# A reordered schedule for a convolution and gated feed-forward kernel: new instruction order, weight sums moved, the last stores split

## The chip, the cores and the metric

The kernel runs on one core of one Trainium2 chip. The metric is the device time of one execution in microseconds, as the median of the runs shown. A core has a matrix engine (TensorE, in the profile PE, with its weight loads as PEld), three engines for elementwise work (VectorE = DVE, ScalarE = ACT, GpSimd = POOL) and queues from which DMA transfers are issued (SP, POOL and ACT issue them here). Each engine works through its own instructions strictly in the order in which the program gave them; between engines there are only semaphore waits. So the order in which the program emits instructions is the schedule.

## What is computed

Everything is in float32.

```
x: (8, 4096, 192), weight: (8 heads, 7 taps), w_gate and w_val: (192, 1536), w_out: (1536, 192), rms_g: (192)

w = softmax(weight, axis=-1)                       # 7 taps for each head of 24 channels
y[b, s, h, :] = sum_k w[h, k] * x_pad[b, s + k, h, :]      # causal, padded with 6 zero rows
t = y.reshape(32768, 192)
tn = t / sqrt(mean(t * t, -1) + 1e-6) * rms_g
g = tn @ w_gate
out = (g * sigmoid(g) * (tn @ w_val)) @ w_out
```

## The kernel before

**Pairs.** The 32768 tokens are cut into 32 pairs of blocks; a pair is 1024 tokens, two halves of 512. Pair 0 is done in the plain way, pairs 1 to 31 with a scheme that saves multiplications: instead of the products of a plain block matrix multiplication, sums of operands are multiplied and the results are added and subtracted again. For this the operands of x (`x_op`, tiles `xb` and their sums `xc`), of w_gate and w_val (`wf`) and of w_out (`wo_sb` and its sums) have to be formed.

**A pair from 1 on** takes 180 steps of TensorE ("places" in the text). The first 120 come from `CHAINS`: for each of four quarters (`Unit` u = 0 to 3) of the 1536 hidden columns, 15 products, each for two halves of the array (gate rows and value rows); line L823, 240 matmuls of 512 columns in all. The other 60 come from `OUTS` ("9.2" is product 9 of quarter 2): they multiply the gated hidden columns, or sums of them, with the forms of w_out; line L1002, eight short matmuls for a step, 480 in all. `LEFT` says which form a product reads and into which accumulator it goes: K, R, N, and C0, C1, C3, C4, which share two PSUM banks. `BANKS` says in which half of the eight banks each of them is.

**The order by hand.** `ORDER` is a list of words, walked once for each pair: "p3" emits the next three products of TensorE, any other word one instruction (or one group) on the engine that its first letter names: A = ScalarE, V, P and W = VectorE, G = GpSimd, Q = an accumulating DMA issued by GpSimd, D = DMAs from SP. A word with a trailing "-" belongs to the pair before. The words:

- `S..`, `F..`, `D5`, `C`, `N`, `R.` with half and quarter: snapshots, forks and joins of the products in PSUM (lines L772, L776, L839, L849, L857); `G.`: the silu (L869); `M.`: the gated product gate x value into `ht` (L877, on GpSimd or VectorE).
- `ab`, `cb`, `de`, `p4`, `p9`, `abe`, `bcf` and so on with a quarter: sums of gated columns (L1027; as Q a DMA, L1025). A `k` in front (`kp9`) stages the second operand in a PSUM bank by ScalarE (L726), so that VectorE (P) can do the sum.
- `X0` to `X10`: the sums `xc` of the next pair's operands (L718; as Q two DMAs, L711 and L712); `fetA`, `fetB`: the DMAs that bring these operands, `xb` (L702), with the small DMA `mark` between them.
- `cv0_1` and so on: tap 0 of 7 in third 1 of the convolution for the pair after the next (ScalarE L474 for tap 0, VectorE L482 for taps 1 to 6); they accumulate in a PSUM bank whose half `SIDE` gives. Then `sq`, `red`, `pow`, `bc`, `mul` (square, reduction on VectorE, root on GpSimd, spread on VectorE, scaling on GpSimd, L498 to L536), `place` (the scaled rows go to DRAM, L676) and `load` (x of a later pair, L158).
- `S2` to `S13`, `F0` to `F4`, `D0` to `D13` without a quarter: snapshots, forks and joins of the output accumulators (L772, L776, L1049); `T0` to `T5`: transposes into `o_sb` (L1015); `st0`, `st1`: the stores, four DMAs each (L1068).

At the end of a pair, joins and transposes are done in the next pair (the words with "-"). For the last pair the walk goes on once more with no pair of its own (`range(1, PAIRS + 1)`, `now = None`).

**The start.** `START` is a string in which each letter advances one generator of pair 0's work: "p", "s", "v" the plain products (L1110), silus (L1121) and gated products (L1128); "i" the conversion of w_gate and w_val (the inputs are float64 words, taken apart), "o" and "O" that of w_out (L335 and L336 are its last two steps, on GpSimd); "c", "n", "t" convolution, norm and `place` of pair 1; "w" the weight sums `w_sums` (L375, and L371 for the two negations of a quarter: 17 sums and 2 negations of 128 columns each, four to a step, five steps to a quarter). `LATER` puts more of these steps at times after `base`, the start of pair 0's output stage `outer` (L1151, evacuated by L1159 on ScalarE and L1163 on VectorE). The numbers are places in an emission order, not clock times: everything is kept in a heap and emitted in the order of these numbers. In the same heap are, for pair 2, the taps: the third accumulator's first tap (L474) at base + 1140, its six further taps (L482) up to base + 1640; then the sums `xc` of pair 1 (L718) from base + 1860 on; and `out_sums`, the 17 sums and one negation of w_out's forms (L914, L910), 12 steps from base + 2600 on and the other six inside pair 1, one after every tenth product.

Of the kernel before, what the change touches and what calls it, by code (L numbers as in the profile page):

```python
# [13 lines left out]
ALU = mybir.AluOpType  # L14
# [5 lines left out]
def kernel(  # L20
# [10 lines left out]
    nc = tc.nc  # L31
# [59 lines left out]
    BANKS = {'K': 1, 'R': 1, 'N': 0, 'C01': 1, 'C34': 0}  # L91
    OUTS = (
        "11.1 11.0 6.0 6.2 4.1 6.1 6.3 11.2 4.2 1.0 1.2 11.3 4.0 4.3 14.3 9.0 8.0 8.1 8.2 9.1 9.3",
        "9.2 14.2 14.1 5.0 8.3 10.0 5.3 10.3 5.1 5.2 3.1 13.2 13.1 3.3 7.0 7.3 13.0 10.1 7.1 10.2",
        "7.2 13.3 1.3 14.0 12.0 3.0 2.1 12.1 12.3 12.2 1.1 3.2 0.3 2.2 2.0 0.1 0.2 2.3 0.0",
    )
    ORDER = (
        "VD6- VD0- GX5- GX10- p1 VT2- p1 GX9- VD2- VD3- VT4- p2 VT5- Asq- AS40.0.0 p2 AS40.1.0",
        "VT3- p1 AF0.0.0 VT0- GX8- p1 VT1- VC.0.0 GX7- AF0.1.0 p3 VC.1.0 AS41.0.0 AS41.1.0 p1",
        "AS00.0.0 p2 AS00.1.0 p2 GX4- p1 Vred- VD5.1.0 AS42.0.0 VD5.0.0 p1 AS42.1.0 VR1.0.0",  # L100
        "VR0.0.0 Gpow- VR1.1.0 AS51.0.0 p1 AS51.1.0 p1 VR0.1.0 p1 Dload- Vbc- AF2.0.0 p1 AG0.0.0",
        "AF3.0.0 AG1.0.0 VN.1.0 p1 VR2.0.0 GM0.1.0 p1 AF3.1.0 p2 AG2.0.0 AS44.1.0 VR2.1.0 p2",
        "Dst1- p1 VS44.0.0 p1 VR3.0.0 p2 AS40.0.1 VR3.1.0 AS40.1.1 p1 GM1.1.0 VR5.0.0 Gmul-",
        "AG4.0.0 GM2.1.0 VR5.1.0 VM4.1.0 AG3.0.0 p1 AF0.0.1 p1 GM3.1.0 p2 Gcb.0 p1 VS41.0.1 p1",
        "AF0.1.1 VC.0.1 p1 AS41.1.1 VC.1.1 AS00.1.1 AG5.0.0 p1 VS00.0.1 p2 AS42.1.1 VS42.0.1",
        "VD5.0.1 AS51.0.1 p1 VD5.1.1 GM5.1.0 p1 AS51.1.1 p1 Gab.0 p2 VR1.0.1 p1 VR1.1.1 p1",
        "AF2.0.1 p1 AF2.1.1 VR0.0.1 p1 VR0.1.1 AG0.0.1 Qbe.0 VF3.0.1 Gdf.0 p3 VR2.0.1 GM0.1.1 p1",
        "AF3.1.1 VR2.1.1 p1 AG1.0.1 AS44.0.1 AS44.1.1 p1 VR5.0.1 AG5.0.1 GM1.1.1 p1 VR3.0.1 p1",
        "AS40.0.2 p2 VR5.1.1 VS40.1.2 p1 VR3.1.1 p2 Gde.0 p3 AG4.0.1 GM5.1.1 AF0.0.2 VM4.1.1",
        "VF0.1.2 AG3.0.1 VC.0.2 AS41.0.2 p2 VC.1.2 AS41.1.2 AG2.0.1 p1 AS00.0.2 p1 VS42.0.2 Gab.1",  # L110
        "p1 GM3.1.1 AS00.1.2 AS42.1.2 p2 VD5.0.2 p4 VD5.1.2 VR1.0.2 AS51.0.2 GM2.1.1 p1 VR1.1.2",
        "AS51.1.2 p2 VR0.0.2 AF2.0.2 p1 AF2.1.2 p1 VR0.1.2 p1 AG1.0.2 AG0.0.2 AF3.1.2 Gcb.1 p1",
        "VF3.0.2 VR2.0.2 VR2.1.2 AS44.0.2 p1 Gdf.1 Qde.1 GM1.1.2 VR5.0.2 AS44.1.2 VR5.1.2 p3",
        "AG2.0.2 p4 VR3.0.2 VS40.1.3 GM0.1.2 AS40.0.3 AG5.0.2 AG4.0.2 VR3.1.2 p1 AF0.0.3 p1",
        "AS41.0.3 p2 Gab.2 VM4.1.2 VF0.1.3 VC.0.3 p1 GM2.1.2 p1 VC.1.3 AS41.1.3 p4 GM5.1.2",
        "VS42.0.3 p1 AS00.0.3 AS00.1.3 VD5.0.3 VD5.1.3 p1 AG3.0.2 Gcb.2 AS42.1.3 p1 VR1.0.3",
        "VR1.1.3 p1 Dst0- AS51.0.3 AS51.1.3 p1 Gdf.2 Gp4.1 AF2.0.3 p1 AF2.1.3 AG1.0.3 VR0.0.3 p1",
        "VR0.1.3 p2 AF3.0.3 AF3.1.3 VS44.0.3 VR5.0.3 p1 GM3.1.2 p1 AG0.0.3 p1 AS44.1.3 VR2.0.3 p2",
        "VR5.1.3 AG5.0.3 p2 Qde.2 VR3.0.3 Qbe.2 AG4.0.3 VM4.1.3 p1 WR3.1.3 AG2.0.3 AG3.0.3 p1",
        "Akp4.2 p2 GM1.1.3 VM3.1.3 p2 GM0.1.3 Akab.3 Akp9.0 Pp4.2 p2 AS6 GM5.1.3 Pab.3 p1 WR2.1.3",  # L120
        "Gdf.3 Dplace- Akp4.0 Gde.3 Acv0_1 p2 DfetA DfetB p1 Pp4.0 p1 AF3 Gp4.3 Akp9.1 VM2.1.3",
        "Qp9.2 p1 Pp9.0 Vcv1_1 Pp9.1 Gcb.3 p1 Gp9.3 p1 Vcv2_1 AF1 p1 Vcv3_1 Vcv4_1 p2 Akabe.1",
        "Akbe.1 Vcv5_1 p1 Pabe.1 p2 Gabe.0 Gabe.2 p2 AF0 Acv0_2 Vcv6_1 p1 Qbe.3 p1 Pbe.1 p1",
        "Vcv1_2 Akbce.0 p1 Qabe.3 p1 VS8 p3 AkX3 p1 Pbce.0 p1 AS5 Vcv2_2 p1 Gbce.3 Akbcf.1 Vcv3_2",
        "PX3 p1 Gbce.2 p2 Gbce.1 Vcv4_2 p1 Vcv5_2 Vcv6_2 Acv0_0 Gbcf.0 QX0 Vcv1_0 Akabd.1 p2",
        "Pbcf.1 Qabd.0 p2 AS7 Pabd.1 p2 Vcv2_0 Gbcf.2 p1 AS13 p2 Akbcf.3 Pbcf.3 VD13 AkX6 Akabd.2",
        "p2 Qabd.3 p1 Vcv3_0 Vcv4_0 Pabd.2 Vcv5_0 p2 AF4 p1 Vcv6_0 p2 VD1 p1 GX1 p3 VD7 AS2 PX6",
        "GX2",
# [238 lines left out]
    def w_sums(u):  # L367
        t = wf[u]
        for i, (d, op, a, b) in enumerate(WSUM):
            if op == "neg":  # L370
                nc.gpsimd.tensor_scalar(  # L371
                    out=t[:, d, :], in0=t[:, a, :], scalar1=-1.0, scalar2=None, op0=ALU.mult
                )
            else:
                nc.gpsimd.tensor_tensor(  # L375
                    out=t[:, d, :], in0=t[:, a, :], in1=t[:, b, :],
                    op=ALU.add if op == "add" else ALU.subtract,
                )
            if i % 4 == 3:
                yield  # L380
        yield
# [524 lines left out]
    def out_sums():  # L906
        for d, op, a, b in VSUM:
            dst = right(d)
            if op == "neg":
                nc.gpsimd.tensor_scalar(  # L910
                    out=dst, in0=right(a), scalar1=-1.0, scalar2=None, op0=ALU.mult
                )
            else:
                nc.gpsimd.tensor_tensor(  # L914
                    out=dst, in0=right(a), in1=right(b),
                    op=ALU.add if op == "add" else ALU.subtract,
                )
            yield

    SIDE = (1, 0, 0)  # L920
# [29 lines left out]
    class Pair:  # L950
# [78 lines left out]
        def do(self, eng, name):  # L1029
# [29 lines left out]
            elif act in ("st0", "st1"):  # L1059
# [4 lines left out]
                for i in range(NQ):  # L1064
                    rows = slice(r + i // 2 * HALFT, r + (i // 2 + 1) * HALFT)
                    cols = slice(i % 2 * D // 2, (i % 2 + 1) * D // 2)
                    q = nc.scalar if i % 2 and p == PAIRS - 1 else nc.sync
                    q.dma_start(  # L1068
                        out=out[rows, cols].rearrange("(b p) d -> p b d", p=Q),
                        in_=o[i * Q : (i + 1) * Q],  # L1070
                    )
# [154 lines left out]
    def done(it):  # L1226
# [11 lines left out]
        "iwpvsicwpsiwvpisvivcpsocvpwispvswcipvwsipsiwOvpsiwvipsvvpswopsvcpsvOnovoOpsonvOpsnoOvnopso"  # L1238
# [3 lines left out]
        (463, "w"), (564, "w"), (664, "w"), (764, "w"), (864, "w"), (964, "w"), (1064, "w"),  # L1242
        (1164, "w"), (1264, "w"),
# [75 lines left out]
    later(wsum, *[base + 2600 + 60 * i for i in range(12)])  # L1319
# [4 lines left out]
    order = [w for row in ORDER for w in row.split()]  # L1324
    past = None
    for p in range(1, PAIRS + 1):
        now = Pair(p) if p < PAIRS else None
        done_to = 0
        for w in order:
            if w[0] == "p":  # L1330
                for _ in range(int(w[1:])):
                    if now:
                        next(now.line)
                    done_to += 1
                    if p == 1 and done_to > 30 and done_to % 10 == 0:
                        next(wsum, None)
# [36 lines left out]
```

## Time and profile before

| | us |
|---|---|
| median of 3 runs | 2606.48 (2603.78 to 2611.65) |
| the profiled execution | 2604.78 |
| its span, first to last instruction | 2602.9 |
| pair 0: first plain product to the end of its output stage | 28.57 to 125.3 |
| pair 1: first L823 to the first L823 of pair 2 | 125.0 to 212.3 |
| pairs 2 to 30 | 212.36 to 2516.61 |
| pair 31: to the end of its last matmul | 2516.61 to 2595.25 |
| mean of one L823 / L1002 matmul as listed | 0.59 / 0.38 |
| one sum of 128 x 512 on GpSimd / on VectorE, as listed | 1.38 to 1.53 / 0.68 |
| one weight sum L375 / L914 on GpSimd, mean | 0.729 / about 0.78 |
| one negation L371 on GpSimd, mean | 0.850 |

A listed duration holds the time in the pipeline; instructions that follow each other without a wait start closer together than that (VectorE's 0.68 at 0.60, GpSimd's 1.27 at 1.23), and matmuls overlap. TensorE's granted clock is 0.999 over the whole run. The 16 DMA engines are busy 40 to 57% of the time in the steady pairs.

### The profile page before, as it was taken

To read this page: it belongs to the slowest core of one execution; us is meant where nothing else is said; L and a number is where in the kernel's file an instruction comes from. 1 tells how busy PE (TensorE), PEld (TensorE's weight loads), DVE (VectorE), ACT (ScalarE), POOL (GpSimd) and SP (SyncE) were. 2 spreads that over 40 slices of the span, in tenths; PEclk is the share of its full clock that TensorE was granted. 3 is DMA by queue.
4 is the path that set the end of the run, shared out by engine and by line. 5 is a ranking of instruction groups with operands and counts; after the bars stand their busy time and mean duration, and the time that the engine had idled before them with its cause. 6 is when DMAs were issued, how large, how long until landed. Compare 5 with 4: busy or idle time off the path is not lost.

```text
span 2602.9 us, 61832 instructions
## 1 busy us (share of the span) xinstructions
PE 2564.1 (99%) x23128; PEld 1467.9 (56%) x23128; DVE 2424.1 (93%) x4056; ACT 1877.9 (72%) x3505; POOL 2398.9 (92%) x2104
## 2 busy tenths in 40 slices
PE   9999999999999999999999999999999999999998
PEld 6855555655555556555555555655556555645554
DVE  8889999999999999999999999999999999999976
ACT  6577777777777777677777777777778777787765
POOL 4899999999999999899999999999999999999987
PEclk9999999999999999999999999999999999999999
DMA  6243554444544445444455444455444455443432
GB/s 144 57 81 67 104 97 87 85 77 90 104 91 82 79 75 104 92 86 87 72 98 104 90 81 76 81 104 96 88 85 77 89 104 91 82 83 71 90 78 50
DMA packets 528490, 226.28 MB, mean 87 GB/s; under 512 B 456638, under 2 KB 459198, under 8 KB 528190
## 3 DMA queue, kind: packets, MB, share of 16 engines
q1 hardware_dynamic: 481004, 140.53, 27.4%
q0 software_dynamic: 44496, 81.02, 18.5%
q8 instruction: 182, 2.98, 0.5%
q10 hardware_dynamic: 2690, 0.79, 0.1%
q14 instruction: 118, 0.97, 0.1%
HBM read 83.84 MB, written 49.55 MB: 51 GB/s over the span
## 4 chain that ended last, share of the span: by engine, by line
PE 71%; POOL 15%; DMA 5%; issue 3%; DVE 2%; ACT 2%; SPq 0%; POOLq 0%; DVEq 0%; ACTq 0%
PE ps L823 51%; PE ps L1002 16%; POOL ht L877 5%; POOL nt L1027 3%; POOL early L1027 3%; PE ps L1110 2%; DMA early<-ht 2%; DMA more<-early 2%; PE ps L1151 1%; POOL tls L1027 1%; DMA xb<-xd 1%; POOL more L1025 1%; POOL more L1027 1%; ACT ps L772 0%; ACT ps L726 0%
## 5 line engine op out<-in xcount | busy, mean ns | idle before, releaser
L823 PE MATMUL ps<-xc,wf 64*128 64x512 f32 x4960 | 1398.1, 592 | 0.9 <-ACT tile L772 0.8
L823 PEld LDWEIGHTS ps<-xc,wf 64*128 64x128 f32 x4960 | 683.2, 187 | 462.4 <-issue 269.6
L823 PE MATMUL ps<-xb,wf 64*128 64x512 f32 x2480 | 864.9, 590 | 0.0
L772 ACT ACTIVATE tile<-ps 128x512 f32<-128x512 f32 (+1 forms) x749 | 416.3, 572 | 201.9 <-PE ps L1002 100.1
L823 PEld LDWEIGHTS ps<-xb,wf 64*128 64x128 f32 x2480 | 375.9, 187 | 241.0 <-issue 179.5
L772 ACT ACTIVATE ps<-ps 128x512 f32<-128x512 f32 (+1 forms) x713 | 383.1, 546 | 176.8 <-PE ps L1002 148.2
L772 ACT ACTIVATE tls<-ps 128x512 f32<-128x512 f32 (+1 forms) x615 | 344.1, 572 | 168.7 <-PE ps L1002 83.8
L877 POOL TENSOR_TENSOR ht<-ht,tile 128x512 f32<-128x512 f32 x312 | 438.8, 1471 | 22.0 <-ACT tile L869 21.1
L1002 PE MATMUL ps<-ht,x 128*32 128x256 f32 x5952 | 413.0, 380 | 0.0
L877 POOL TENSOR_TENSOR ht<-ht,tls 128x512 f32<-128x512 f32 x246 | 349.0, 1468 | 22.8 <-ACT tls L869 22.0
L1027 POOL TENSOR_TENSOR early<-early,ht 128x512 f32<-128x512 f32 x248 | 351.3, 1527 | 0.0
L482 DVE SCALAR_TENSOR_TENSOR ps<-xh,tp,ps 128x512 f32<-128x512 f32 x450 | 337.3, 751 | 15.1 <-ACT ps L474 8.8
L1027 POOL TENSOR_TENSOR early<-ht 128x512 f32<-128x512 f32 x248 | 342.7, 1382 | 4.8
L1002 PE MATMUL ps<-early,x 128*32 128x256 f32 x4216 | 278.9, 379 | 0.1
L1002 PEld LDWEIGHTS ps<-ht,x 128*32 128x32 f32 x5952 | 192.1, 110 | 130.1 <-DVE ht L877 4.9
L857 DVE TENSOR_TENSOR tile<-ps,tile 128x512 f32<-128x512 f32 x344 | 233.0, 684 | 11.0 <-ACT tile L772 6.3
L869 ACT ACTIVATE tile<-tile 128x512 f32<-128x512 f32 x344 | 213.9, 625 | 7.6 <-DVE tile L857 4.4
L857 DVE TENSOR_TENSOR ht<-ps,tile 128x512 f32<-128x512 f32 x310 | 209.9, 680 | 0.7 <-ACT tile L772 0.5
L857 DVE TENSOR_TENSOR tls<-ps,tls 128x512 f32<-128x512 f32 x276 | 187.3, 684 | 8.6 <-ACT tls L772 5.0
L726 ACT COPY ps<-ht 128x512 f32<-128x512 f32 x248 | 145.3, 589 | 60.2 <-DVE y L482 44.9
L1002 PEld LDWEIGHTS ps<-early,x 128*32 128x32 f32 x4216 | 136.6, 110 | 91.9 <-ACT ps L772 5.0
L869 ACT ACTIVATE tls<-tls 128x512 f32<-128x512 f32 x276 | 171.8, 625 | 6.0 <-DVE tls L857 3.6
(174 smaller groups left out, 3897.3 us busy)
## 6 DMA issues: line engine op xcount, KB each, us to landing
xb<-xd SPq DMA_DIRECT2D x120, 384.0 KB
ht<-ht POOLq DMA_DIRECT2D x93, 256.0 KB, 3.9
early<-ht POOLq DMA_DIRECT2D x93, 256.0 KB, 4.6
xd<-yn SPq DMA_DIRECT2D x244, 96.0 KB
out_dram<-o_sb SPq DMA_DIRECT2D x244, 96.0 KB
xh<-in_x_dram SPq DMA_DIRECT2D x192, 105.0 KB
more<-ht POOLq DMA_DIRECT2D x62, 256.0 KB, 3.3
more<-early POOLq DMA_DIRECT2D x31, 256.0 KB, 3.9
```

The costliest lines, as they stand in the source:

```text
L482: nc.vector.scalar_tensor_tensor(out=dst, in0=xk, scalar=w, in1=at, op0=ALU.mult, op1=ALU.add)
L726: nc.scalar.copy(out=bank(*at)[:], in_=src)
L772: nc.scalar.activation(out=dst, in_=src, func=AF.Copy, scale=float(s))
L823: nc.tensor.matmul(out=self.new(v, h, True) if first else self.old(v, h), lhsT=wf[self.u][HALF[h], WAT[i], :], rhs=x_op(XOP[i])[HALF[h]], ...
L857: nc.vector.tensor_tensor(out=dst, in0=self.old(v, h), in1=t[:], op=plus(s))
L869: nc.scalar.activation(out=t[:], in_=src[:], func=AF.Silu)
L877: engine[eng].tensor_tensor(out=self.hv(v), in0=src, in1=t[:], op=ALU.mult)
L1002: nc.tensor.matmul(out=to[q * Q : (q + 1) * Q, :], lhsT=left[:, u, a], rhs=cols[:, i * HALFT : (i + 1) * HALFT], start=fresh, stop=True, s ...
L1025: nc.gpsimd.dma_start(out=dst, in_=b, accum_op=ALU.add)
L1027: engine[eng].tensor_tensor(out=dst, in0=a, in1=b, op=ALU.add)
L1110: nc.tensor.matmul(out=bank(h, bks[h])[:], lhsT=wf[u][HALF[h], AT[h][k] * NF + f, :], rhs=xb[HALF[h], g, k, :], start=(k == 0), stop=(k == ...
L1151: nc.tensor.matmul(out=bank(h, bks[h])[:, w : w + D], lhsT=hts[f // NF][HALF[h], g, f % NF, j * P : (j + 1) * P], rhs=wo_sb[HALF[h], f, :] ...
```

## The change

The words of ORDER and OUTS are replaced throughout. Beside that:

- `BANKS` puts accumulators K and R into the other half, `SIDE` puts all three convolution accumulators of a pair from 3 on into the upper half.
- Several words change their engine. Sums: `p4.0`, `ab.3`, `abe.1`, `bcf.1`, `p9.2`, `de.1` and `X0` go to GpSimd; `cb.3`, `de.3`, `df.3`, `abe.2`, `abe.3`, `bcf.2` and `abd.0` to VectorE with staging; `de.0`, `be.1`, `abd.2`, `bcf.3` become DMAs. The gated products `M5` of quarters 2 and 3 go from GpSimd to VectorE.
- `fetA` moves from place 131 to 138 and `fetB` from 131 to 156; `place` from 129 to 69; `load` from 21 to 12; `st1` of the pair before from 28 to 152, between `fetA` and `fetB`; `st0` from 108 to 83.
- The two negations of each quarter of `w_sums`, and the one of `out_sums`, are done by ScalarE instead of GpSimd.
- START gets four more "w" (so that three quarters of the weight sums stand in it, not two and a fifth of the third), LATER has five instead of nine, the last at base + 864.
- All 18 steps of `out_sums` are emitted in pair 0's output stage: seven from base + 964, eight from base + 2520, three from base + 2910.
- For the last pair a new function `last` rewrites the order: each join, transpose, snapshot `S2` and store is emitted at once when what it needs (`NEEDS`) has been emitted, not in a walk after the pair; only `st1` still uses ScalarE's queue for half of its DMAs. The additional walk is gone.

```diff
-    BANKS = {'K': 1, 'R': 1, 'N': 0, 'C01': 1, 'C34': 0}
+    BANKS = {'K': 0, 'R': 0, 'N': 0, 'C01': 1, 'C34': 0}
     OUTS = (
-        "11.1 11.0 6.0 6.2 4.1 6.1 6.3 11.2 4.2 1.0 1.2 11.3 4.0 4.3 14.3 9.0 8.0 8.1 8.2 9.1 9.3",
...
-        "7.2 13.3 1.3 14.0 12.0 3.0 2.1 12.1 12.3 12.2 1.1 3.2 0.3 2.2 2.0 0.1 0.2 2.3 0.0",
+        "6.2 4.1 4.0 6.0 11.2 11.1 6.1 6.3 11.0 4.2 1.0 11.3 1.2 1.1 14.3 4.3 9.2 9.1 9.0 8.2 8.1",
...
+        "3.3 1.3 14.0 14.1 2.1 3.1 10.0 12.0 12.2 12.1 12.3 10.2 2.3 2.0 2.2 0.3 0.0 0.1 0.2",
     )
     ORDER = (
...
-        "p2 Qabd.3 p1 Vcv3_0 Vcv4_0 Pabd.2 Vcv5_0 p2 AF4 p1 Vcv6_0 p2 VD1 p1 GX1 p3 VD7 AS2 PX6",
-        "GX2",
+        "AkX3 AF4 GX0 Vcv5_2 PX3 p3 Vcv5_0 AkX6 AS2 p1 GX1 p2 Vcv6_0 VD7 Vcv6_2 GX2 PX6 GX5 p1",
+        "VT2 GX10 VD6",
     )
...
             if op == "neg":
-                nc.gpsimd.tensor_scalar(
-                    out=t[:, d, :], in0=t[:, a, :], scalar1=-1.0, scalar2=None, op0=ALU.mult
-                )
+                nc.scalar.mul(t[:, d, :], t[:, a, :], -1.0)
...
-    SIDE = (1, 0, 0)
+    SIDE = (1, 1, 1)
...
-        "iwpvsicwpsiwvpisvivcpsocvpwispvswcipvwsipsiwOvpsiwvipsvvpswopsvcpsvOnovoOpsonvOpsnoOvnopso"
+        "iwpvsicwpsiwvpisvivcpsocvpwispvswcipvwsipsiwOvpsiwvipsvvpswopsvcpsvOnovowOpsonwvOpsno"
+        "wOvnopswo"
...
-        (463, "w"), (564, "w"), (664, "w"), (764, "w"), (864, "w"), (964, "w"), (1064, "w"),
-        (1164, "w"), (1264, "w"),
+        (463, "w"), (564, "w"), (664, "w"), (764, "w"), (864, "w"),
...
-    later(wsum, *[base + 2600 + 60 * i for i in range(12)])
+    later(wsum, *[base + 964 + 80 * i for i in range(7)])
+    later(wsum, *[base + 2520 + 40 * i for i in range(8)])
+    later(wsum, *[base + 2910 + 10 * i for i in range(3)])
...
+    NEEDS = {
+        "D6": "F4 S6", "D0": "S8 F0", "D2": "S2 F4", "D3": "S2 F3", "D1": "S5 F1",
+        "D13": "S13 S6", "D7": "S7 S6", "T0": "3 D0", "T1": "10 D1", "T2": "1 D13 D7",
+        "T3": "14 D3", "T4": "0 F4", "T5": "F4 D2 D6", "st0": "T0 T1 T2", "st1": "T3 T4 T5",
+        "S2": "2",
+    }
...
+    for p in range(1, PAIRS):
+        now = Pair(p)
+        if p == PAIRS - 1:
+            order = last(order, " ".join(OUTS).split())
...
-                    if p == 1 and done_to > 30 and done_to % 10 == 0:
-                        next(wsum, None)
+                    next(now.line)
```

## The prediction

> **What bounds the kernel now.** I read the page's busy shares first, then the chain of waits in order of time, then what TensorE waited for, then timelines of one steady pair, of the first pair and of the end.
>
> ```profile
> span 2602.9 us, 61832 instructions
> PE 2564.1 (99%) x23128; PEld 1467.9 (56%) x23128; DVE 2424.1 (93%) x4056; ACT 1877.9 (72%) x3505; POOL 2398.9 (92%) x2104
> ```
>
> TensorE is 99% busy, so a new order can win only what TensorE loses; but VectorE and GpSimd stand above 90% too, so it can lose more than it wins. The chain shows each pair's first product (columns: start, length, what).
>
> ```profile
> 1005.58 37.40 PE ps L823 x170
> ...
> 1065.07 7.15 DMA more<-early
> 1072.26 17.04 PE ps L1002 x312
> 1089.30 37.19 PE ps L823 x171
> ...
> 1168.34 51.78 PE ps L823 x239
> ```
>
> From start to start this gives the pairs: 83.72 us here, then 79.04. All 29 from 212.36 to 2516.61 take 2304.25 us, 79.46 each. The 13 shortest lie at 78.74 to 79.04, mean 78.88, and in ten of them no transfer is among the chain's longest pieces; in 14 of the other 16 one is (without the 83.72 they average 79.67). The work alone is 51.78 for the 240 L823 and 480 L1002 at 17.04/312, 26.2: 78.0 us, 0.433 us for each of the 180 products ("places") of a pair. What TensorE itself waited for:
>
> ```profile
> PE ps L1002 <- POOL nt L1027: 9.8, 32, 1.3
> PE ps L1002 <- DMA more<-early: 7.1, 6, 3.0
> PE ps L1002 <- DMA early<-ht: 5.3, 8, 0.9
> ```
>
> The first is sum `p9.3` on GpSimd (0.24 us at 988.04), the others are accumulating DMAs `p9.2` and `abd.3`/`abe.3` that land late.
>
> **The steady pairs.** A DMA is safe if it is issued long before the product that reads it. Counting places in ORDER and OUTS, the shortest distances before are 7 (`de.2`), 8 (`p9.2`), 8 (`abd.3`), 10 (`be.2`); after they are 8 (`be.2`), 12, 14 (`bcf.3`), 14 (`abd.3`), 20. In the trace GpSimd runs contiguously and its real issue counts: `p9.2` is issued at 984.44, its product was due at 988.25, 3.8 us later, where the landing's median is 3.9; `abd.3` at 999.22, due at 1004.5, 5.3 against 5.1 to 6.0 on the chain. After, `p9.2` is a GpSimd sum; `bcf.3` and `abd.3` gain six places, less one or two for the queue in front, some 2 us: beyond the 6.0. `X0` becomes a GpSimd sum instead of two transfers.
>
> What this costs on GpSimd: in ORDER it has 50 sums and 9 DMA issues instead of 49 and 10. Back to back a sum takes 1.233 us (six from 967.13 to 974.54), a DMA issue about 0.75: +0.5 us a pair, against 2.3 us that it idles before the factors and the first gated product. Can it still reach `p9.3` in time?
>
> ```profile
> 936.86 1.28 POOL L877 TENSOR_TENSOR ht<-ht,tile 128x512 f32<-128x512 f32 x1 [1.25 <-ACT tile L869]
> ...
> 986.70 1.29 POOL L1027 TENSOR_TENSOR nt<-nt,early 128x512 f32<-128x512 f32 x1
> ```
>
> Before, from 936.86 to the end of `p9.3` at 987.99 are 34 sums, 5 issues and the scaling: 51.1 us. After, the same 34, 5 and the scaling stand between the start of the scaling and the end of `p9.3`. The scaling waits for VectorE's `bc`, which stands six instructions of 0.60 behind `red` (930.88, 4.2 into the pair, 2.2 long): 4.2 + 2.2 + 3.6 = 10.0. So `p9.3` ends at 61.3, and its product, one place later than before, is due at 141 x 0.433 + 0.3 = 61.4: its 0.24 us goes. `X10`, which the second product needs, then ends 12 sums and 4 issues later, 79.1 us, due at 79.9.
>
> VectorE has two sums fewer and two gated products more, ScalarE two stages fewer; both are near even. The store `st1` now stands between the halves of the fetch on SP's queue; the fetched half before it landed in 6.9 us (978.52 to 985.38), and the first use moves from place 155 to 173, 7.8 us later, which hides it. The new banks add waits that no row shows: between nothing and the 0.44 that the worst `p9.3` wait of a steady pair cost. I take nothing, because a bank is freed by rows that are already just in time.
>
> I take 78.95 a pair: the mean of the 13 shortest, with 0.07 for what is left of late transfers. 2304.25 - 29 x 78.95 = **14.7 us gained**. Ends: 78.6 (the shortest of all, the last pair: 2595.25 - 2516.61) gives 24.9; 80.26, the longest ordinary pair, costs 23.3.
>
> **The first pair.** It takes 212.36 - 125.0 = 87.4 us, 8.0 above a steady one. Six weight sums L914 of 0.73 to 1.02 push GpSimd back by some 5 us, until TensorE stands at 190.7 for the DMA behind them.
>
> ```profile
> 193.73 1.08 PE L1002 MATMUL ps<-more,wo_sb 128*32 128x256 f32 x8 [2.98 <-DMA more<-early]
> ```
>
> After, all 18 are queued before the pair begins. If the pair then runs like the others, it gains the **8.0**. But pair 0 pays. Here is GpSimd, then ScalarE, then VectorE there:
>
> ```profile
> 101.19 2.89 POOL L536 TENSOR_TENSOR yn<-y,s 128x1536 f32<-128x1536 f32 x1
> 103.96 6.52 POOL L375 TENSOR_TENSOR wf<-wf 128x128 f32<-128x128 f32 x13
> ...
> 111.54 10.49 POOL L375 TENSOR_TENSOR wf<-wf 128x128 f32<-128x128 f32 x17
> ```
>
> ```profile
> 107.64 0.69 ACT L474 ACTIVATE ps<-xh,tp 128x512 f32<-128x512 f32 x1 [7.39 <-POOL wf L375]
> ```
>
> ```profile
> 108.37 3.92 DVE L482 SCALAR_TENSOR_TENSOR ps<-xh,tp,ps 128x512 f32<-128x512 f32 x5 [0.70 <-ACT ps L474]
> ```
>
> Four more steps of `w_sums` in START put 13 sums ahead of the last conversions of w_out: 13 x 0.617 = 8.0, of which idle gaps of 2.42 and 1.96 take 4.4; GpSimd reaches L536 3.6 us later (2.1 with the 0.50 of the row at 103.96). Then come the sums of the last quarter, whose two negations are now on ScalarE, at emission time base + 864, and must wait for its 15th sum: 104.08 + 3.6 + 15 x 0.617 = 116.9 (113.7 with 0.50). Behind them in ScalarE's order is L474 at base + 1140, until now at 107.64. VectorE's third tap chain moves from 108.37 by 9 us (6), and behind it stand the sums L718 that end at 125.8 and that the first products of pair 1 need. So pair 1 starts 5.5 to 9 us later; I take 7. A TensorE that stood still also runs slower: after the 2.98 us above, 32 matmuls took 2.92 us (194.59 to 197.51) instead of 1.73, and the granted clock was 0.90 there: 1.2 us. Removing eight negations of 0.85 from GpSimd is in these figures. Net: 7 + 1.2 - 8.0, about **0**; ends -8 (the wait is covered after all) and +4.
>
> [...]
>
> **The end.** After the last matmul (2594.64 + 0.61) come a snapshot, joins and five transposes, until 2597.87, and then stores.
>
> ```profile
> 2594.89 0.38 ACT L772 ACTIVATE tile<-ps 128x256 f32<-128x256 f32 x1 [3.09 <-PE ps L1002]
> 2595.30 0.76 DVE L1049 TENSOR_TENSOR ps<-ps,tile 128x256 f32<-128x256 f32 x2 [1.23 <-ACT tile L772]
> 2596.10 1.77 DVE L1015 STREAM_TRANSPOSE o_sb<-ps 128x256 f32<-128x256 f32 x5
> 2597.24 2.10 SPq L1068 DMA_DIRECT2D out_dram<-o_sb  x4
> ```
>
> After, bank R ends four places earlier (2593.5); snapshot 0.38, two joins 0.75 and two transposes 0.8 run beside the last products to 2595.5, the last transpose ends at 2595.9, and `st0` has left already. **2.0 us gained**; ends 1 (a join waits in VectorE's order) and 3.
>
> **The sum.** -14.7 + 0 - 2.0 = -16.7 on the profiled execution's 2604.78 us (span 2602.9 and 1.9 around it): 2588.1. The median, 2606.48, is 1.7 above that execution, so I forecast **2590 us**, with 2583 to 2598 as this case's own range (steady part 8 to 20).
>
> **Rivals.** (A) Everything fits: pairs at 78.6 and the first pair's 8.0 kept: -24.9 - 8 - 2 = 2571.6 by the median. For it: the last pair does 78.64; against: only the last one, with fewer transfers. 12%.
> (B) The waits only move: GpSimd and VectorE stay above 90%, another transfer becomes the late one, the steady pairs stay at 79.46. -2.0: 2604.5. For it: `be.2` has still 8 places, and the load is the same. 22%.
> (C) Slower: VectorE becomes the bound at the start of each pair. In ORDER `cv6_0` and `cv6_2` now stand with `PX6` at place 179; before, `PX6` ended 0.14 us ahead of the first product (1005.44 against 1005.58). If VectorE runs on plan and not ahead of it, the two tap steps of 0.66 delay each pair's first product by 1.3: 29 x 1.3 = 37.7 instead of nothing, less the 14.7 and 2.0: +21, 2627. It turns slower as soon as the delay is above 0.6 us a pair. Against it: from place 166 on VectorE has 10 instructions, 5.8 us, in 14 places of 6.1 us. 16%.
> The forecast has 50%. Medians of this kernel spread so that 0.3%, 7.8 us, is about what can be told from no change: faster is below 2598.7, slower above 2614.3. The forecast lies almost wholly below, with A: 62%; B and the forecast's edge 22% the same; C 16%. The range 2573 to 2614 leaves out half of A and most of C.
>
> **What would show it.** Pair starts 78.9 apart with no `early<-ht` or `more<-early` in front of L1002 confirm the steady part; 79.4 or more means B, a wait of L823 for L718 at pair starts C. ScalarE idle before L474 near 107, and TensorE idle between L1151 and L823 near 125 to 133, confirm pair 0's price; a first pair of about 79 us its gain. The last transpose should end within 1 us of the last matmul. A steady pair above 79.3 makes the prediction wrong.

## The result, and the profile after

Timed against each other, the kernel before takes 2603.68 us (median of 12 runs) and the changed one 2608.22 (12 runs): a ratio of 1.0018, with a 95% interval of 1.0010 to 1.0025. The change costs 0.2%. The forecast was a gain of 0.6%; the loss is smaller than the 0.3% that it named as hard to tell from no change, but the interval leaves no change out.

The head of the profile after: the span, then each engine's busy time, share and instructions.

```profile
span 2607.2 us, 61944 instructions
PE 2574.3 (99%) x23128; PEld 1582.0 (61%) x23128; DVE 2427.4 (93%) x4025; ACT 1848.7 (71%) x3483; POOL 2399.5 (92%) x2095
```

The engines' shares say nothing: they are those of before. What TensorE waited for says more (columns: total us, times, longest):

```profile
PE ps L820 <- POOL xc L715: 10.6, 29, 0.4
PE ps L997 <- DVE o_sb L1010: 2.9, 2, 2.4
PE ps L820 <- DVE o_sb L1158: 2.7, 1, 2.7
PE ps L997 <- DMA ht<-ht: 2.3, 1, 2.3
```

(After the change L823 is L820, L1002 is L997, L718 is L715, L1027 is L1022, L1015 is L1010, L1163 is L1158.) The waits of the output phase are gone: before there were 9.8 us for sums of GpSimd and 12.4 for accumulating DMAs; one transfer is left. In their place stands a wait of 0.37 us in nearly every pair, for a sum of `xc` on GpSimd. Here is TensorE, then GpSimd, around the start of one pair:

```profile
769.24 1.13 PE L820 MATMUL ps<-xc,wf 64*128 64x512 f32 x4
770.74 1.13 PE L820 MATMUL ps<-xc,wf 64*128 64x512 f32 x4 [0.38 <-POOL xc L715]
771.71 1.02 PE L820 MATMUL ps<-xb,wf 64*128 64x512 f32 x4
```

```profile
750.75 1.27 POOL L1022 TENSOR_TENSOR nt<-nt,early 128x512 f32<-128x512 f32 x1
751.98 0.82 POOL L1020 DMA_DIRECT2D ht<-ht  x1
752.59 4.00 POOL L1022 TENSOR_TENSOR early<-early,ht 128x512 f32<-128x512 f32 x3
756.32 1.11 POOL L1020 DMA_DIRECT2D early<-ht  x1
756.92 3.05 POOL L1022 TENSOR_TENSOR early<-early,ht 128x512 f32<-128x512 f32 x2
759.39 2.31 POOL L1020 DMA_DIRECT2D early<-ht  x2
760.53 3.71 POOL L1022 TENSOR_TENSOR early<-early,ht 128x512 f32<-128x512 f32 x2
763.03 2.44 POOL L715 TENSOR_TENSOR xc<-xb 128x512 f32<-128x512 f32 x1
765.55 2.55 POOL L715 TENSOR_TENSOR xc<-xb,xc 128x512 f32<-128x512 f32 x2
768.04 2.65 POOL L715 TENSOR_TENSOR xc<-xc 128x512 f32<-128x512 f32 x2
```

The first row is `p9.3`. The last four groups are `X0`; `X1` and `X2`; `X5` and `X10`. `X10` ends at 770.69, and TensorE's second product, which reads it, starts at 770.74: 1.50 us behind the first. In the kernel before, and in the kernels below that have `X10` early, this distance is 0.96. So 0.54 us is lost here, of which the profile shows 0.38 as idle, because the modelled end of the first four matmuls covers the rest.

From the first product of each pair in the two timelines, the time between kernels divides like this:

| part | forecast | measured |
|---|---|---|
| start of pair 2 (212.29 before, 213.70 after) | 0 | +1.4 |
| 29 steady pairs (2304.26, 2306.52) | -14.7 | +2.3 |
| start of pair 31 to the span's end (86.35, 86.98) | -2.0 | +0.6 |
| span (2602.9, 2607.2) | -16.7 | +4.3 |

Single traces differ: with those of the experiments below, the old order's 29 steady pairs take 2304.25 to 2307.95 us in three traces, the new order's 2305.58 to 2309.31 in seven. Between them lies nothing like the 14.7 that were forecast.

A pair's product phase is the time from its first L820 to its first L997, its output phase the rest. A steady pair now has an output phase of 26.3 us, almost always (before 26.4 to 27.9, and once 31.2), and a product phase of 53.07 (before 52.19 to 52.72). What the first won, the second gave back.

### The profile page after: what moved, and what is told of

Same layout as the page of the kernel before. It is cut to its first block, busy times and chain, and to the rows that moved or that the text cites. A ratio compares the mean times of both kernels' runs of the same rounds, so it can differ in the third digit from the quotient of the medians.

```text
span 2607.2 us, 61944 instructions
## 1 busy us (share of the span) xinstructions
PE 2574.3 (99%) x23128; PEld 1582.0 (61%) x23128; DVE 2427.4 (93%) x4025; ACT 1848.7 (71%) x3483; POOL 2399.5 (92%) x2095
## 3 DMA queue, kind: packets, MB, share of 16 engines
q8 instruction: 182, 2.98, 0.5%
## 4 chain that ended last, share of the span: by engine, by line
PE 90%; POOL 6%; issue 1%; DVE 1%; ACT 1%; DMA 0%; POOLq 0%; DVEq 0%
PE ps L820 59%; PE ps L997 28%; POOL xc L715 3%; PE ps L1105 2%; POOL ht L874 1%; POOL early L1022 1%; PE ps L1146 1%; DVE xc L715 0%; DMA ht<-ht 0%; POOL more L1022 0%; ACT tls L769 0%; POOL wf L372 0%; POOL early L1020 0%; POOL tls L1022 0%; POOL nt L1022 0%
## 5 line engine op out<-in xcount | busy, mean ns | idle before, releaser
L820 PE MATMUL ps<-xc,wf 64*128 64x512 f32 x4960 | 1433.7, 595 | 14.3 <-POOL xc L715 10.6
L820 PEld LDWEIGHTS ps<-xc,wf 64*128 64x128 f32 x4960 | 716.6, 187 | 433.4 <-issue 258.3
L820 PE MATMUL ps<-xb,wf 64*128 64x512 f32 x2480 | 886.7, 589 | 0.0
L820 PEld LDWEIGHTS ps<-xb,wf 64*128 64x128 f32 x2480 | 394.6, 187 | 189.8 <-issue 152.5
L769 ACT ACTIVATE tls<-ps 128x512 f32<-128x512 f32 x681 | 375.8, 566 | 160.7 <-PE ps L820 89.1
L997 PE MATMUL ps<-ht,x 128*32 128x256 f32 x5952 | 391.0, 380 | 5.2 <-DVE o_sb L1010 2.9
L874 POOL TENSOR_TENSOR ht<-ht,tile 128x512 f32<-128x512 f32 x245 | 357.1, 1514 | 31.1 <-ACT tile L866 30.9
L1022 POOL TENSOR_TENSOR early<-early,ht 128x512 f32<-128x512 f32 x217 | 334.8, 1885 | 1.8 <-PE ps L997 1.8
L1022 POOL TENSOR_TENSOR early<-ht 128x512 f32<-128x512 f32 x248 | 322.4, 1348 | 7.3
L997 PEld LDWEIGHTS ps<-ht,x 128*32 128x32 f32 x5952 | 190.0, 110 | 152.3 <-issue 25.8
L997 PE MATMUL ps<-early,x 128*32 128x256 f32 x4216 | 262.3, 380 | 0.0
L854 DVE TENSOR_TENSOR tls<-ps,tls 128x512 f32<-128x512 f32 x314 | 212.9, 684 | 8.9 <-ACT tls L769 3.6
L854 DVE TENSOR_TENSOR tile<-ps,tile 128x512 f32<-128x512 f32 x306 | 205.5, 683 | 4.9 <-ACT tile L769 1.8
L866 ACT ACTIVATE tls<-tls 128x512 f32<-128x512 f32 x314 | 196.2, 625 | 0.0
L997 PEld LDWEIGHTS ps<-early,x 128*32 128x32 f32 x4216 | 133.9, 110 | 95.8 <-POOL early L1022 10.5
L866 ACT ACTIVATE tile<-tile 128x512 f32<-128x512 f32 x306 | 189.5, 626 | 0.0
```

The source lines that it names most:

```text
L769: nc.scalar.activation(out=dst, in_=src, func=AF.Copy, scale=float(s))
L820: nc.tensor.matmul(out=self.new(v, h, True) if first else self.old(v, h), lhsT=wf[self.u][HALF[h], WAT[i], :], rhs=x_op(XOP[i])[HALF[h]], ...
L854: nc.vector.tensor_tensor(out=dst, in0=self.old(v, h), in1=t[:], op=plus(s))
L866: nc.scalar.activation(out=t[:], in_=src[:], func=AF.Silu)
L874: engine[eng].tensor_tensor(out=self.hv(v), in0=src, in1=t[:], op=ALU.mult)
L997: nc.tensor.matmul(out=to[q * Q : (q + 1) * Q, :], lhsT=left[:, u, a], rhs=cols[:, i * HALFT : (i + 1) * HALFT], start=fresh, stop=True, s ...
```

## Experiments

All were timed in turns with the kernel before, on one chip for each group; the ratios are to it.

**What sets the pair.** Theory: GpSimd's last sums. The rival is VectorE, or the banks.

```diff
- ... p1 GX1 p2 Vcv6_0 VD7 Vcv6_2 GX2 PX6 GX5 p1 VT2 GX10 VD6
+ ... p3 Vcv6_0 VD7 Vcv6_2 GX2 PX6 GX5 p1 VT2 GX10 VD6
- VD1- Asq- VD2- GX8- ... GX9- AS40.0.0
+ VD1- Asq- VD2- GX8- ... GX9- GX1- AS40.0.0
```

> The changed kernel with one GpSimd sum of a pair's end, X1, moved behind X10, X8 and X9 (the product that reads X1 is the tenth of a pair, the one that reads X10 the second). Theory (the last sums of GpSimd set the pair): X10 ends one sum, 1.24 us, earlier; the 0.64 us that TensorE loses ahead of the second product (0.37 of it shown as idle) goes, and as the sums end 79.6 us after the pair's start, just when they are due, the product phase falls from 53.07 to about 52.4 and a steady pair from 79.35 to about 78.7: 29 pairs gain 18, the time is near 2590. Rival 1 (VectorE at the pair's start, sums PX3 and PX6 and the tap steps, or the new banks): the order of GpSimd's sums is not what is waited for; product phase and pairs stay at 53.07 and 79.35, the time at 2608. Rival 2 (the whole loop over VectorE, scaling and GpSimd sets the pair and takes up what is given): a part only, pairs between 79.0 and 79.3.

2589.24 us, ratio 0.9947 (0.9935 to 0.9960); the product phase is 52.42, a steady pair 78.7 and the mean of 29, with one late transfer, 78.89. These are the theory's numbers; both rivals fall. (In this kernel `X5` adds the `X1` of the pair before, because `X1` now follows it, so it doesn't compute the formula. The third kernel of this group has an early `X10` and the whole sum.) The other direction:

```diff
- ... GX2 PX6 GX5 p1 VT2 GX10 VD6
+ ... GX2 PX6 GX5 p1 GX8 VT2 GX10 VD6
- VD1- Asq- VD2- GX8- VT5-
+ VD1- Asq- VD2- VT5-
```

> The changed kernel with one more GpSimd sum, X8, moved ahead of X10 (the same work, X10 one sum later). Theory (TensorE's second product waits for X10, and nothing else takes it up): the wait grows from 0.64 by the sum's 1.24 us, product phase 54.3, pairs 80.6, 29 pairs cost 36 us: 2644. Rival (the loop gives it back, since GpSimd idles 2.2 us before the scaling): pairs below 80.0, the time below 2628.

2641.88 us, ratio 1.0143 (1.0129 to 1.0157); pairs of 80.5, mean 80.68, product phase 54.18. This is TensorE's wait in that kernel:

```profile
939.93 1.13 PE L820 MATMUL ps<-xc,wf 64*128 64x512 f32 x4 [1.48 <-POOL xc L715]
```

1.1 us more on the wait for a sum of 1.24 more ahead of it. Nothing downstream takes it up: `red` starts 5.9 us into a pair here, 4.8 in the changed kernel, so the whole chain that leads to the next `X10` shifts with the late product; the idle time that GpSimd has (0.81 us before the factors, 1.42 before the scaling in the pair from 689.87) lies at another place of the pair and can't help.

`X10` can also come early with `X1` still ahead of `X5`: `X3`, on which `X5`, `X6` and `X10` build, goes into the place of `X9`, so that `X10` no longer overwrites what `X5` reads:

```diff
-        (0, 1, 4), (1, 2, 6), (2, 0, 6), (9, 3, 5), (3, 3, 8), (4, 7, 15), (5, 4, 15), (6, 5, 7),
-        (7, 0, 1), (8, 1, 2), (9, 8, 15),
+        (0, 1, 4), (1, 2, 6), (2, 0, 6), (8, 3, 5), (3, 3, 8), (4, 7, 14), (5, 4, 14), (6, 5, 7),
+        (7, 0, 1), (8, 1, 2), (9, 8, 14),
- ... GX1 p2 Vcv6_0 VD7 Vcv6_2 GX2 PX6 GX5 p1 VT2 GX10 VD6
+ ... GX2 p2 Vcv6_0 VD7 Vcv6_2 GX10 PX6 GX1 p1 VT2 GX5 VD6
```

> The changed kernel with X10 third among GpSimd's last sums (X0, X2, X10, X1, X5) and the whole sum kept: X3, on which X5, X6 and X10 build, goes into the place of X9, which is summed later, so X10 no longer overwrites what X5 reads. Theory (the last sums of GpSimd set the pair): X10 ends 2.5 us earlier, at 78.3 after the pair's start; X5 takes the end at 80.8, and the fourth product, which reads it, is due 2.6 us after the next start, at 81.3; so no wait is left at the start: product phase 52.4, pairs 78.7 to 78.9, the time 2589 to 2592. Rival (what X1 left out of its place gave was an effect of the data, or the loop takes the gain back): pairs above 79.1, the time above 2600.

2592.05 us, ratio 0.9946 (0.9933 to 0.9959), mean pair 78.94, product phase 52.43. With the changed kernel at 1.0018, the place of one sum is worth 0.7%.

**Which part of the change costs what.** Each part alone, put into the kernel before:

```diff
+ BANKS, OUTS and ORDER of the changed kernel
-    SIDE = (1, 0, 0)
+    SIDE = (1, 1, 1)
```

> The kernel before with the new steady order alone (ORDER, OUTS, BANKS, SIDE); first pair and last pair in the old way. Theory: output phases of 26.3 without a wait for a transfer, product phases of 53.07; the steady part is 2 us longer than before (29 x 79.5), the start of pair 2 as before (212), the last pair 0.7 longer by the same wait at its start: +2 to +4 us on the kernel before. If it gains more than 5 us, the loss of the changed kernel comes from the first or the last pair.

2603.34 us, ratio 0.9993 (0.9984 to 1.0001). The steady pairs are as foretold (mean 79.50, product phase 53.07), and the end is 87.27 against 86.35. The surprise is the beginning: pair 2 starts at 206.94, 5.3 us earlier than before, though nothing of the first pair's own sums was touched. Pair 1 takes 82.19 instead of 87.29. Part of this is chance in the trace of before: the last kernel of this group has the old first pair and the old order too, its pair 1 takes 83.93 us, and its pair 2 starts at 209.68, because TensorE waits 1.5 us for one DMA there and not 3.0, and its granted clock isn't halved behind that wait (before: 0.50 from 193.6 to 197.0). So pair 2 starts 2.7 to 5.3 us earlier by the new order.

```diff
+ START, LATER and places of `out_sums` of the changed kernel
-                nc.gpsimd.tensor_scalar( ... scalar1=-1.0 ... )
+                nc.scalar.mul( ... , -1.0)
```

> The kernel before with the changed first pair alone (START, LATER, the places of the weight sums, negations on ScalarE). Theory: pair 0 ends 4 to 5 us later because ScalarE's third tap waits behind two negations for GpSimd, pair 1 runs 3 us shorter; with the old order, whose first output phase then has no weight sum ahead of its transfers, pair 2 starts 0 to 2 us later than before, the rest is unchanged: 0 to +2 us. Rival (the forecast's other end): pair 1 runs at the steady 79.5 and the whole gains 3 us or more.

2611.02 us, ratio 1.0025 (1.0016 to 1.0034). Pair 1 starts at 129.17 (125.00 before), pair 2 at 214.86 (212.29); the rest is as before. The median lies beyond what these 2.6 us explain. But against the 209.68 of the other trace with the old first pair and order, pair 2 starts 5.2 us later; and the profiled run, 2607.53 us, is one of the shorter ones. The rival, a gain, falls.

```diff
+    def last(order, outs): ...
-    for p in range(1, PAIRS + 1):
+    for p in range(1, PAIRS):
```

> The kernel before with the changed last pair alone (joins, transposes and stores at once). Theory: TensorE stands before products 10 and 0, which write the other half of a bank that a transpose still reads, some 2 to 3 us in all (2.9 in the changed kernel), so the last matmul comes that much later, and the end is between 0.5 us earlier and 1 us later than before. Rival (the forecast): transposes run beside the last products and the end comes 2 us earlier.

2606.00 us, ratio 1.0006 (0.9997 to 1.0015): no gain. From the start of pair 31 to the end it takes 86.57 us, 0.2 more than before, and TensorE stands 1.98 us for a transpose ahead of its last product.

**The last pair.** This is the end of the changed kernel in its timeline, all engines: the snapshot `S2` on ScalarE, on VectorE `D2`, `T5`, `D3` and `T3`, and TensorE's last four products behind `T3`:

```profile
2598.40 0.38 ACT L769 ACTIVATE tile<-ps 128x256 f32<-128x256 f32 x1 [1.36 <-PE ps L997]
2598.82 0.43 DVE L1044 TENSOR_TENSOR ps<-ps,tile 128x256 f32<-128x256 f32 x1 [0.94 <-ACT tile L769]
2599.28 0.45 DVE L1010 STREAM_TRANSPOSE o_sb<-ps 128x256 f32<-128x256 f32 x1
2599.66 0.40 DVE L1044 TENSOR_TENSOR ps<-ps,tile 128x256 f32<-128x256 f32 x1
2600.09 0.45 DVE L1010 STREAM_TRANSPOSE o_sb<-ps 128x256 f32<-128x256 f32 x1
...
2600.69 1.93 PE L997 MATMUL ps<-ht,x 128*32 128x256 f32 x32 [2.35 <-DVE o_sb L1010]
```

`C3` and `C4` are halves of one bank (`C34`). As soon as product 2 is through, `last` queues the join `D3` and the transpose `T3` on `C3`; product 0, which writes `C4`, comes behind them and waits for both.

```diff
- ... "D3": "S2 F3", ... "T0": "3 D0", ... "T3": "14 D3", ...
+ ... "D3": "S2 F3 0", ... "T0": "3 D0 10", ... "T3": "14 D3 0", ...
```

> The changed kernel with three joins and transposes of the last pair (T0, D3, T3) held back until the products of the other half of their bank are through. Theory: TensorE's waits of 0.57 and 2.35 us ahead of the last products go, the last matmul comes 2.9 us earlier, the transposes then follow it; the end is 1 to 2.5 us earlier than in the changed kernel. Rival (the wait for a transpose is not for the bank): the 2.35 stays before the last products and the end moves less than 0.5 us.

2607.96 us, ratio 1.0001 (0.9992 to 1.0010), where the changed kernel has 1.0018. Both waits are gone, and from the start of pair 31 it takes 84.70 us instead of 86.98: 2.3 less, as the theory has it. The waits of 0.57 and 2.35 us were two products' waits for a transpose in the other half of their bank; whether the chip itself would need them was not tried.

**The first pair.** This is ScalarE at the end of pair 0 in the changed kernel:

```profile
107.12 3.49 ACTq L673 DMA_DIRECT2D xd<-yn  x4
114.31 0.51 ACT L370 ACTIVATE wf<-wf 128x128 f32<-128x128 f32 x2 [11.06 <-POOL wf L372]
114.73 0.67 ACT L471 ACTIVATE ps<-xh,tp 128x512 f32<-128x512 f32 x1
117.56 0.42 ACT L907 ACTIVATE x<-x 128x256 f32<-128x256 f32 x1 [2.16 <-POOL x L909]
117.88 0.46 ACT L1154 COPY o_sb<-ps 128x384 f32<-128x384 f32 x1
120.17 1.48 ACT L495 ACTIVATE yn<-y 128x1536 f32<-128x1536 f32 x1 [1.83 <-DVE y L479]
```

Two negations (L370) wait for GpSimd's 17 sums, and the third tap (L471), VectorE's tap chain, the square (L495) and the sums `xc` of pair 1 wait behind them. Four edits take this apart. First, the last step of the weight sums, with its negations, behind the tap:

```diff
-        ... (764, "w"), (864, "w"),
+        ... (764, "w"), (1150, "w"),
```

> The changed kernel with the step that holds the last quarter's two negations (and the sum before them) emitted behind ScalarE's third tap instead of ahead of it. Theory: the tap starts when its DMA issues end, near 110.6 instead of 114.7, VectorE's third tap chain 4 us earlier, pair 1 starts at 125 to 126.5 instead of 129.6 and pair 2 some 3 to 4 us earlier: 2604 to 2606. Rival (GpSimd's weight sums themselves, which run beside VectorE's sums, set pair 1): pair 1 starts no more than 1.5 us earlier, or pair 2's start moves less than 1.5 us.

2608.37 us, ratio 1.0004 (0.9994 to 1.0015). The tap starts at 111.41, but pair 1 only 1.6 us earlier and pair 2 too. That is just beyond the rival's 1.5 and far from the theory's 3 to 4; and five traces with the changed first pair as it is start pair 1 at 129.02 to 130.44 and pair 2 at 212.78 to 214.16, so this is little more than their spread. Now the other negation (L907) stood in front: it waited for GpSimd until 117.92, and the copy L1154 and the square (118.60) waited behind it. Next, the output weights' sums at their old places, their negation on GpSimd:

```diff
-    later(wsum, *[base + 964 + 80 * i for i in range(7)])
-    later(wsum, *[base + 2520 + 40 * i for i in range(8)])
-    later(wsum, *[base + 2910 + 10 * i for i in range(3)])
+    later(wsum, *[base + 2600 + 60 * i for i in range(12)])
```

> The changed kernel with the 18 sums of the output weights (and their one negation, on GpSimd) at their old places in pair 1; the sums of the first weights stay moved up. Theory (pair 1's slow start, a wait of 2.67 us for VectorE's o_sb, comes from the moved sums, which run beside VectorE's sums at 1.05 to 1.17 us instead of 0.72 while those take 1.10 to 1.20 instead of 0.68): VectorE's sums take 0.7 to 0.9 again, the wait of 2.67 goes, pair 1's product phase falls from 57.6 to about 54.5 and pair 2 starts at 210 to 212 instead of 213.7. Rival (only the late third tap counts): the wait stays above 2 us, pair 2 starts at 213.5 or later.

2612.19 us, ratio 1.0029 (1.0018 to 1.0040). A miss for my theory: the wait is 2.38 us, pair 2 starts at 215.55, as the rival says. The moved output sums rather help, by 1.9 us between these two traces. That VectorE's sums run beside GpSimd's in this order too, since both start late, behind the square (119.54), is my estimate; how long they take in this kernel is not shown here. Then the opposite half, the first weights' sums and negations as before, the output weights' as changed:

> The changed kernel with the sums of the first weights at their old places and their negations on GpSimd again; the output weights' sums stay moved up. Theory (the 13 weight sums ahead of pair 2's scaling and the two negations ahead of ScalarE's third tap make pair 1 late): the third tap starts before 109 us, pair 1 starts at 125 to 127.5 and pair 2 at 206 to 210 instead of 213.7: 2601 to 2605. Rival (any work moved into pair 0 costs about the same): pair 1 starts after 128.5, pair 2 after 212.

2612.55 us, ratio 1.0026 (1.0017 to 1.0035): against the theory again. The tap starts early (107.20), as it said, but the one negation left on ScalarE waits, and the rest waits behind it:

```profile
107.20 0.69 ACT L473 ACTIVATE ps<-xh,tp 128x512 f32<-128x512 f32 x1 [7.56 <-POOL wf L374]
118.86 0.42 ACT L909 ACTIVATE x<-x 128x256 f32<-128x256 f32 x1 [10.96 <-POOL x L911]
119.18 0.46 ACT L1156 COPY o_sb<-ps 128x384 f32<-128x384 f32 x1
119.54 1.49 ACT L497 ACTIVATE yn<-y 128x1536 f32<-128x1536 f32 x1
```

So either negation alone makes the square late. The last edit undoes all of them and nothing else:

```diff
-                nc.scalar.mul( ... , -1.0)
+                nc.gpsimd.tensor_scalar( ... scalar1=-1.0 ... )
```

> The changed kernel with all eight negations back on GpSimd and every sum left at its new place. Theory (each of the negations alone, queued on ScalarE ahead of the third tap or ahead of its copy into o_sb and the square, makes VectorE's sums and so pair 1 late; with one of them left, pair 1 started at 129.0 and 129.7): the third tap starts near 110.6, the square near 116 instead of 120.2, pair 1 at 125.5 to 127.5 and pair 2 at 208 to 211 instead of 213.7; the time is 3 to 5 us below the changed kernel's. Rival (the moved sums themselves make GpSimd, and so pair 1, late): pair 1 starts after 128.5, pair 2 after 212.5.

In the profile the theory's numbers come, or nearly: square 117.05, pair 1 at 127.58, pair 2 at 209.96, 3.7 us earlier. The median does not show it: 2607.19, ratio 1.0018 (1.0009 to 1.0027), as the changed kernel's. Single runs go from 2604.28 to 2614.14, and the profiled one, 2604.78, is among the three with a granted clock of 1.00; the two longest have 0.997. So the gain is shown in one trace and not in the time.

And 1.7 of its 3.7 us are the clock. In the changed kernel pair 1's product phase is 57.59 us, here 55.89. Both have the same wait of 2.67 us, for VectorE's `o_sb`, ahead of the seventh matmul. Behind it the granted clock is 0.50 from 135.5 to 138.9 us in the changed kernel, and 1.00 here. That is not tied to the negations: `e1_x1`, the first kernel of these experiments, has the changed first pair with its negations on ScalarE and that wait, and there too the clock stays at 1.00 and the phase is 55.89. The same 14 matmuls behind the wait, in the changed kernel and in `e1_x1`:

```profile
136.41 4.77 PE L820 MATMUL ps<-xc,wf 64*128 64x512 f32 x14
```

```profile
136.81 3.52 PE L820 MATMUL ps<-xc,wf 64*128 64x512 f32 x14
```

Together (the last column says for how long the granted clock is 0.50 in pair 1):

| kernel | square | pair 1 | pair 2 | half clock |
|---|---|---|---|---|
| old first pair, new order | 112.98 | 124.75 | 206.94 | none |
| all sums moved, no negation on ScalarE | 117.05 | 127.58 | 209.96 | none |
| first negations behind the tap | 118.60 | 128.04 | 212.13 | 3.41 |
| only first weights moved | 119.54 | 128.98 | 215.55 | 3.41 |
| only output weights moved | 119.54 | 129.72 | 213.67 | 3.41 |
| changed kernel | 120.17 | 129.60 | 213.70 | 3.41 |

Of the 6.8 us between the first and the last row, 2.0 are the later start of pair 1 that goes with the negations, and 1.7 the clock. The other 3.0 come with the moved sums; no kernel here moves the sums of one kind alone and leaves ScalarE without a negation. The rows point at the 13 weight sums: GpSimd's scaling (100.92 in the first kernel, 104.78 in the second) and ScalarE's third tap behind it are 3.9 and 4.1 us later.

**What beats both.** The new order with the early `X10`, and the old first and last pair:

> The kernel before with the new steady order and the early X10 of the run before this one, first and last pair in the old way. Theory: the steady gain (18 us on the steady order alone, 2603.3) without the 6.8 us by which the changed first pair starts pair 2 later: 2585, about 0.7% below the kernel before. Rival (the old first pair's weight sums collide with the earlier X10): above 2589.

2584.51 us, ratio 0.9911 (0.9897 to 0.9924). With the mended last pair as well:

> The new steady order with the early X10, the first pair in the old way, and the last pair with T0, D3 and T3 held back. Theory: the 2584.5 of the kernel without the last pair's change, less 1 to 2 us at the end: 2583. Rival: the last pair's change gives nothing, 2584.5 or more.

2581.31 us, ratio 0.9908 (0.9893 to 0.9924); the last part takes 84.09 us in place of 86.74. In the steady part this is all that the view of TensorE's waits lists, 2.4 us:

```profile
PE ps L1001 <- POOL tls L1026: 1.6, 2, 0.9
PE ps L1001 <- DMA ht<-ht: 0.8, 1, 0.8
```

With the moved sums instead of the old first pair:

> The same with the early X10 and the held back joins and transposes of the last pair: the changed kernel with its three losses mended. Theory: 18 us for the steady pairs, 2 for the end and 3 to 5 for the first pair: 2582 to 2586. It beats the version with the old first pair (2581.3) only if pair 2 starts before 207.6.

2587.17 us, ratio 0.9937 (0.9924 to 0.9950): pair 2 starts at 213.54. The moved sums don't pay in this order either. Pair 1's product phase is 58.92 here, and 55.89 with the same first pair in the changed order: behind the same wait of 2.67 us the granted clock is 0.50 for 6.83 us, from 132.3 to 139.1. Without these 3.0 us pair 2 would start near 210.5 (an estimate from these two phases), still later than the 207.60 of the kernel with the old first pair.

## Why the prediction was wrong

**The steady pairs.** The gain in the output phase was right, with its mechanism: DMAs with more places ahead of their product no longer come late (TensorE waited 12.4 us for them before, 2.3 after), and `p9.3`'s 0.24 goes. The step that failed is the next: "`X10`, which the second product needs, then ends 12 sums and 4 issues later, 79.1 us, due at 79.9." In the pair from 689.87 it ended at 80.8, and with pairs of 78.7 it was due at 79.7 (78.7 + 0.96). The terms, one by one:

- The scaling was put at 10.0 us into the pair, and came at 10.94 (700.81): `red` starts 4.8 us into a pair (774.04 in the next) instead of 4.2, behind VectorE's joins. But these joins wait for the products that the late `X10` has held up at this pair's own start. In the kernels with an early `X10` `red` starts at 4.16, as forecast, and the scaling at 10.30. So of the 0.9 only 0.3 is the forecast's error, and 0.6 is the loss itself.
- From there to the end of `p9.3`: forecast 51.3, measured 51.2. Right.
- From there to `X10`: forecast 17.8, measured 18.7 (752.02 to 770.69). Twelve sums at 1.233 are 14.8, so the four DMA issues cost 3.9, 0.97 each and not 0.75. My 0.75 was read from the distance between an issue's start and the next start; but after an issue the rows overlap (two sums shown as 3.71 us, the next starting 2.50 behind them), and the time shows later: here at `X0`, 2.44 us long where the sums before the first issue take 1.27, with `X1`, which reads it, 2.52 behind it. This is 0.9. That `X0` is the place because `X1` needs its result is my reading of these rows.

So without a loss at the pair's own start `X10` would end at 80.2 (10.30 + 51.2 + 18.7), 0.5 later than due, and 0.54 is what the second product loses. Of the 1.1 us between this and the forecast's 79.1, the four DMA issues are 0.9: they are the mis-sized term. The margin of 0.8 us, on which 29 pairs hung, was smaller than this error alone. It had no term of its own in the range: the forecast said "no loss", where 1 us too late would have cost 29 us. The rest of this sum holds: where `X10` is early, the mean pair is 78.89 to 78.94, and 78.95 was forecast.

**Banks** were put at nothing, "freed by rows that are already just in time", with 0.44 as the other end. Where `X10` is early, the product phase is still 52.43 against 52.19. In the changed kernel and in these, two weight loads of a pair wait for VectorE: one some 13 us into the pair, 0.20 us, and one some 43 us into it, 0.36 in the changed kernel; the matmuls behind them are 0.07 and 0.15 us later. So some 0.2 us a pair, 6 in all, lies between the two ends. That the new banks cause these waits is not shown: the old banks under the new order were not tried.

**Rivals.** C had the place (a wait at each pair's start) and the point from which the time turns slower, 0.6 us a pair: measured 0.88 on the product phase, and the steady part is 2.3 us longer. It named the wrong engine and price: GpSimd's `X10`, not VectorE's tap steps with 1.3. The forecast's sign "a wait of L823 for L718" came, from the other engine. The sign "above 79.3" came too (79.53 as the mean).

**The first pair** came out at +1.4 inside its ends of -8 and +4, by errors that cancel. The wait of ScalarE was foreseen; the negations were put at 116.9 and ran at 114.31, since the last quarter's 17 sums took 0.493 us each and not 0.617. Pair 1 started 4.6 us later instead of 7. But of the 8.0 that pair 1 was to win, the new order takes 1.7 to 5.1 without the sums' move (82.19 us against 83.93 and 87.29), which the forecast had not asked; the changed pair 1 took 84.10. Against the new order alone the moved sums and negations lose 6.8 us, 1.7 of it by the clock. The forecast had a term for that, 1.2, read from before's trace with a mean clock of 0.90; over the stretch that it names, 194.59 to 197.51, the clock is 0.59 there, and over 193.6 to 197.0 it is 0.50.

The row from which the prediction took 0.617 for a weight sum holds two speeds. In the kernel before, 11 of the 17 weight sums fall into the 5.4 us up to 116.9, 0.49 each; then VectorE's sums `xc` begin, and the other six take 5.1 us, up to 122.0, 0.84 each. So 0.617 is their mean. In the changed kernel VectorE does taps (`ps<-xh,tp,ps`) or waits beside these 17 sums, and all of them take 0.493. The output sums show two speeds too, below.

**The end** had its mechanism right but left out that two products wait for a transpose in the other half of their bank, 0.57 and 2.35 us in the changed kernel. Its -2.0 became +0.6, of which 0.7 is the same `X10` ahead of the last pair; with the waits gone the last part is 1.7 us shorter than before (84.70 against 86.35), though its product phase still holds the wait for `X10`.

## What to carry to other kernels

When an order takes a late transfer off the path, ask what each engine finishes last before the stage starts again, and at which instruction; a margin of 0.8 us that rests on a sum of 50 rows is no margin, and belongs into the range times the number of stages. An instruction moved to an idle engine waits there in order: what is queued behind it (here a tap, a copy and a square, at 114.73, 117.88 and 120.17 us, and at 111.58, 112.21 and 117.05 with no negation on ScalarE) pays for its input, so the engine's idle time is not the price. Test a part of a change against the rest of that change, too: a part that looked like a small loss beside the old order was worth 6.8 us beside the new one. And read one trace as one draw: the clock behind the same wait halved in some executions and not in others, at 1.7 us each time, and an old trace's late transfer passed for a price of the first pair.

## What the runs showed of the hardware

A DMA issue on GpSimd costs 0.97 us of its time from 752.02 to 770.69 us of the changed kernel, not the 0.6 to 0.75 between its row's start and the next: of 18.67 us, twelve sums leave 3.9 for four.

TensorE's granted clock was 0.50 behind some waits, for 3.41 us or twice that: behind 2.98 us in the kernel before (from 193.6), behind 2.67 (135.5) and 2.32 (2101.6) in the changed one, for 6.83 us behind 2.67 in the last kernel of the experiments. Behind the same 2.67 us in two other kernels it stayed at 1.00. A stretch of 3.41 costs 1.7 us (57.59 against 55.89).

GpSimd's sums and VectorE's sums `xc` slowed each other in these traces. Between 127.8 and 133.9 us of the changed kernel the two are GpSimd's output sums and VectorE's `xc`:

```profile
115.31 0.72 POOL L909 TENSOR_TENSOR x<-wo_sb 128x256 f32<-128x256 f32 x1
...
127.75 1.16 POOL L909 TENSOR_TENSOR x<-wo_sb 128x256 f32<-128x256 f32 x1
```

```profile
126.89 0.68 DVE L715 TENSOR_TENSOR xc<-xb 128x512 f32<-128x512 f32 x1
...
130.51 2.34 DVE L715 TENSOR_TENSOR xc<-xb 128x512 f32<-128x512 f32 x2
```

0.72 becomes 1.16, and 0.68 becomes 1.17, at once. Beside VectorE's taps this does not show: from 115.43 on five of them take 3.92 us, as in the kernel before (108.37), and the output sums there still take 0.72. In strict turns a pair of sums, one on each engine, would take 1.28 us, by the distances between starts without the other engine's sums (0.68 on GpSimd, 0.60 on VectorE); 1.13 was measured, from start to start on either engine. So they come near taking turns, but are a little faster than that.
